# Moving early VectorE products to GpSimd and ScalarE, a later token weight, and w spread by a transfer, in a fused linear-attention and mixer kernel

## The chip, the cores and the metric

The kernel runs on one core of one Trainium2 chip. The metric is the device time of one execution in microseconds. Engine names are those of the profile: PE is TensorE (PEld its weight loads), DVE VectorE, ACT ScalarE, POOL GpSimd, SP SyncE, which only issues transfers here.

## The reference

Inputs r, k, v are (4 batches, 8 heads, 768 tokens, 48), w and u are (8, 48), all float32. A linear attention with decay runs over the tokens, and a mixer follows on its output:

```
for t in range(S):
    cur = einsum('bhd,bhe->bhde', u * k[t], v[t])
    y[t] = einsum('bhd,bhde->bhe', r[t], state + cur)
    state = w * state + einsum('bhd,bhe->bhde', k[t], v[t])
x = y as (B, 768, 384)
h = relu(x^T @ w_tok1) @ w_tok2        # over tokens, 768 -> 256 -> 768
u = x + h^T
out = u + relu(u @ w_ch1) @ w_ch2      # over channels, 384 -> 1536 -> 384
```

## The kernel before, in words

The attention is cut into 24 units of 128 tokens: six chunks of each of four batches. For a unit u the steps are these, by the names in the code:

- `kp`, `rp`: k and r (float32, as loaded) times powers of the decay, `wn` and `wp`, written as bfloat16 into `kpr`. The tables come from ln w: `lnw_` (line 618) takes logarithms of `w_ps` in PSUM into `lnw` (every row of which holds all of w) and `lnr` (r's layout), multiplies `lnr` by indices on DVE, and `wn_`, `wp_` take exponentials on ACT.
- `trk`, `trr`: PE transposes of the k and the r half into one PSUM tile `tr_ps`. `rk` copies both halves to SBUF on ACT after both are transposed; for units in `rk_two` (0 to 4 and 6) the copies are steps of their own, `rkk` behind `trk` and `rkr` behind `trr`.
- `at`: the scores of 8 heads into two PSUM tiles `at_ps` of four heads each. `AT0` and `AT1` multiply them by a causal mask on DVE, from PSUM. For units in `raw` (0, 1, 5, 8, 11) the second one is instead copied to SBUF as bfloat16 by ACT (`raw`) and masked from there (`ATr`).
- `pr`, `pg`, `yd`: the token's own term with u. `yS`, `y`: products with the state and with v, into `y_ps`. `x`: the sum, as `x_b`, read by the mixer. `kv`, `S`: the state; at the half of a batch `S` is multiplied by `wGm`, a product of a block mask `bm` and w to a power.

A planner (`Plan.run`, line 73) places all steps on the engines by assumed costs. The order in which it starts them is the program order; each engine then runs its list in order, and `fill` (line 130) puts idle matmuls into PE's planned gaps of the ramp. `products_in_turn` (line 146) makes some POOL products wait for a DVE step so that the two don't run against each other. The planned engine of `kp2` and `wGm` is DVE; `kp0`, `rp0`, `kp1`, `rp1`, `rp2`, `kp3` and most of the others of the first batch are on POOL.

Loads of the first six units are issued by SP in a fixed order from the start (`first_loads`, line 663), the next ones only after unit 5's y. The weights are transfers from POOL's queue (`weight`, line 694), in program order between its products: `w0` (first token weight) after `kp4`, `w1` (second token weight, `wtok2`) after `rp4`, and behind `rp5` five pieces of the channel weights, `w2`, `w6`, `w4` (first channel weight: a quarter, a quarter, a half), `w3`, `w5` (second channel weight, halves).

Spreading w: at line 536 ACT issues a transfer of w as one row of 384 into `row`, then one of four rows of 96 into `row4`. PE multiplies a column of ones by `row` (line 551) and a selection matrix `quarter` by `row4` (line 556) into `w_ps`, with idle matmuls around them.

The mixer of the first batch starts when its x is done: `hid` (tokens, first weight), `hr` (relu), then `ub` and `bk` with `wtok2`, then `z` with `wch1` in twelve pieces of 128 columns (pieces 0 to 2 read `w2`, 3 to 5 `w6`, 6 to 11 `w4`), `zr`, and `h` with `wch2`. PE's order is fixed by the plan, so a late weight stops PE.

Of the kernel before, what the change touches and what calls it, by code (L numbers as in the profile page):

```python
# [13 lines left out]
f32 = mybir.dt.float32  # L14
# [6 lines left out]
Ln = ACTF.Ln  # L21

B, H, S, D = 4, 8, 768, 48
# [22 lines left out]
class Plan:  # L46
# [83 lines left out]
    def fill(self, since, until, least, margin, each, emit):  # L130

        mine = sorted((s for s in self.steps if s.engine == "PE"), key=lambda s: s.start)
        for a, b in zip(mine, mine[1:]):
            if b.start > until:
                break
            if a.end < since:
                continue
            taken = sum(1 for x in self.used if x[0] < b.start and x[1] > a.end)
            n = int((b.start - a.end - margin) / each)
            if b.start - a.end >= least and taken < self.banks and n > 0:  # L140
                s = self.add(f"fill{a.name}", [("PE", n * each, n * each)], emit=emit(n))
                s.engine, s.start, s.end, s.seen = "PE", a.end, a.end + n * each, a.end + n * each
        return sorted(self.steps, key=lambda s: s.start)


def products_in_turn(steps, apart):


    both = [s for s in steps if s.engine in ("DVE", "POOL") and s.name.rstrip("0123456789") in ("kp", "rp", "ku", "rku", "yd", "wGm")]
    dve = [s for s in steps if s.engine == "DVE"]  # L150
    behind, d = {}, None
    for s in both:
        if s.engine == "DVE":
            d = s if len(s.after) and s.name[:2] != "yd" or s.ways[0][0] == "POOL" else d
        elif d is not None and s.start - d.end < apart:
            n = dve.index(d)
            behind[s] = dve[n - 1] if n and d.start - dve[n - 1].end < 0.05 else d
            d = None
    return behind
# [9 lines left out]
def graph(do, cfg):  # L169
# [246 lines left out]
CFG = dict(apart=2.0,   # L416
    transfers=[("u", u) for u in range(0, 6)]
    + [('k', 6)]
    + [('r', 6)]
    + [('k', 7)]  # L420
    + [('r', 7)]
    + [('v', 6)]
    + [('v', 7)]
    + [('u', 8)]
# [20 lines left out]
    xload={6: 0.33},  # L445
    wtime=(3.0, 2.6, 1.55, 5.2, 3.1, 3.9, 1.55),
    raw=(0, 1, 5, 8, 11),
    rk_two=(0, 1, 2, 3, 4, 6),
    mix=(0.0, 0.0, -1.0, -2.6),
    off3=[{}, {}, {'AT0': -0.12, 'rp': 0.83, 'rku': 1.35}],  # L450
# [17 lines left out]
def kernel(  # L468
# [15 lines left out]
    dm = H * D  # L484
# [8 lines left out]
    const = ctx.enter_context(tc.tile_pool(name="const", bufs=1))  # L493
# [7 lines left out]
    psM = ctx.enter_context(tc.tile_pool(name="psM", bufs=4, space=bass.MemoryType.PSUM))  # L501
# [19 lines left out]
    pe, dve, act, pool, sp = (InOrder(e) for e in (nc.tensor, nc.vector, nc.scalar, nc.gpsimd, nc.sync))  # L521
# [5 lines left out]

    idle = const.tile([128, 512], bf16, name="idle")
    dve.memset(idle, 0.0)
    row = const.tile([1, dm], f32, name="row")  # L530
    row4 = const.tile([HP, 2 * D], f32, name="row4")
    rows = const.tile([2 * HP, 2, P], f32, name="rows")
    dve.memset(rows, 1.0)
    wide = len(by_pe) < NU
    u_bc = const.tile([128, dm], f32, name="u_bc") if wide else None
    act.dma_start(out=row, in_=w.rearrange("h d -> (h d)")[None, :])
    act.dma_start(out=row4, in_=w.rearrange("(a q) d -> a (q d)", q=2))
    act.preload_act_table_set("natural_log_exp_and_others")
    ones = const.tile([1, 128], f32, name="ones")
    dve.memset(ones, 1.0)  # L540


    idle_ps = psM.tile([128, 512], f32, name="idle_ps", tag="m")
    w_ps = psM.tile([128, dm + 2 * D], f32, name="w_ps", tag="m")

    def warm(n):
        for _ in range(n):
            pe.matmul(idle_ps, idle[:, 0:128], idle, start=True, stop=True)

    warm(CFG.get("warm", (1, 10))[0])  # L550
    pe.matmul(w_ps[:, 0:dm], ones, row, start=True, stop=True, skip_group_check=True)
    ident = const.tile([128, 128], bf16, name="ident")
    make_identity(nc, ident)
    quarter = const.tile([HP, T // R, HP], f32, name="quarter")
    dve.tensor_copy(quarter, ident[0:HP, 0:HP].unsqueeze(1).to_broadcast([HP, T // R, HP]))
    pe.matmul(w_ps[:, dm:], quarter.rearrange("p t a -> p (t a)"), row4, start=False, stop=True, skip_group_check=True)
    warm(CFG.get("warm", (1, 10))[1])

    iota_i = const.tile([128, 2, G], i32, name="iota_i")
# [14 lines left out]
        out=mask, in_=mask, compare_op=ALU.is_gt,  # L574
# [15 lines left out]
    for i in range(NB):  # L590
        t = const.tile([128, 2, H, P], bf16, name=f"kpr{i}")
# [13 lines left out]
        dve.memset(S_i, 0.0)  # L605
        S0s.append(S_i)

    lnw = const.tile([128, dm], f32, name="lnw")
    wn = const.tile([128, G, dm], f32, name="wn")
    wp = const.tile([128, G, dm], f32, name="wp")  # L610
    wr = wp.rearrange("p g (q j d) -> p g q j d", q=2, j=R)
    lnr = const.tile([128, 2, D], f32, name="lnr")
# [3 lines left out]
    wGm = const.tile([128, HP, 2, D], f32, name="wGm")  # L616

    def lnw_(eng):
        act.activation(lnw, w_ps[:, 0:dm], Ln)
        act.activation(lnr.rearrange("p q d -> p (q d)"), w_ps[:, dm:], Ln)  # L620
        shape = [128, 2, R, D]
        for g in range(G):
            dve.tensor_mul(wr[:, g], lnr.unsqueeze(2).to_broadcast(shape), iota_r[:, g].unsqueeze(1).unsqueeze(3).to_broadcast(shape))
# [368 lines left out]
    def out_(eng, b, c, part, parts):  # L992
        sp.dma_start(out[b, ts(c, 128), ts(part, dm // parts)], M[b]["o", c, part])

    STEPS = {
        "lnw": lnw_, "wn": wn_, "wp": wp_, "wu": wu, "uw": uw, "ubc": ubc, "load": load, "weight": weight, "gd": gd, "wGm": wgm, "kp": kp, "rp": rp,
        "vb": vb, "ku": ku, "rku": rku, "adg": adg, "yd": yd, "turn_unit": turn_unit,
        "trk": lambda e, i: tr(0, i), "trr": lambda e, i: tr(1, i), "rk": rk, "at": at, "AT": AT, "raw": raw,
# [5 lines left out]
    def do(kind, *args):  # L1004
        return lambda eng: STEPS[kind](eng, *args)

    def fill(eng, n):
        t = psM.tile([128, 512], f32, name="fill_ps", tag="m")
        for lo in range(0, n, 2):
            cols = slice(0, 256 * min(2, n - lo))  # L1010
            pe.matmul(t[:, cols], idle[:, 0:128], idle[:, cols], start=True, stop=True)

    plan = graph(do, CFG)
    steps = plan.run()
    if CFG.get("fill"):
        first = next(s for s in steps if s.name == "z0_0_0").start
        steps = plan.fill(CFG.get("fill_from", 0.0), first, *CFG["fill"], lambda n: lambda eng: fill(eng, n))
    behind = products_in_turn(steps, CFG["apart"])
    last = {}
    for s in steps:  # L1020
# [38 lines left out]
```

## Time and profile before

| what | value |
|---|---|
| time, median of 3 runs | 165.36 us (164.93 to 165.66) |
| time of the profiled execution | 165.7 us |
| its span in the trace | 164.0 us |
| PE busy | 156.6 us (95%) |
| DVE busy | 109.2 us (67%) |
| ACT busy | 88.5 us (54%) |
| POOL busy | 67.1 us (41%) |
| first `z_ps` matmul | 29.94 us after the span's start |

Timeline lines give start, duration, engine, line, operation and tiles, then the count; a bracket holds the idle time before it and what ended it. Nearly all instructions have line 515, the helper that records them, so one goes by tiles: `kpr<-ld_k` is kp, `AT<-at_ps,mask` a masked score product, `AT<-raw,mask_b` the one from SBUF. Rows "A:B" of the stretches give the length, the busy time of PE, PEld, DVE, ACT and POOL (with counts), the granted clock, the DMA share and GB/s. Transfer lines end with the time from issue to landing.

### The profile page before, as it was taken

What the parts mean: (1) busy time and instruction counts of PE and PEld (TensorE: products, weight loads), DVE (VectorE), ACT (ScalarE), POOL (GpSimd) and SP (SyncE); (2) the same over time, 40 slices, a digit from 0 to 9 for tenths busy, and PEclk for the clock granted to TensorE, in tenths of its full rate; (3) what the DMA queues carried; (4) which work ended last, traced back from release to release, by engine and by line L of the source; (5) the groups of instructions that cost most, each with busy time, mean ns of one, the idle gap of its engine ahead of it and who ended that gap; (6) DMA issues with size and microseconds to landing.
All of it is one profiled execution on the core that took longest, in us unless ns stands there. A gap on an engine that the chain in (4) does not pass through costs nothing.

```text
span 164.0 us, 3852 instructions
## 1 busy us (share of the span) xinstructions
PE 156.6 (95%) x1466; PEld 100.9 (62%) x1466; DVE 109.2 (67%) x225; ACT 88.5 (54%) x194; POOL 67.1 (41%) x83
## 2 busy tenths in 40 slices
PE   6798999999999999899999999999999999999992
PEld 3277865566677666566566565666656655666562
DVE  6679897602289889899899899977876582012021
ACT  3898662595488466789706450077253502914900
POOL 8748893000037848566875856204750000000000
DMA  4999999999798997999999972999990028012012
GB/s 92 221 223 207 173 154 173 192 194 232 153 231 233 190 213 220 196 238 180 217 231 133 263 135 67 203 231 194 194 240 4 0 53 216 19 52 96 0 48 96
DMA packets 87307, 26.26 MB, mean 160 GB/s; under 512 B 76665, under 2 KB 87290, under 8 KB 87290
## 3 DMA queue, kind: packets, MB, share of 16 engines
q1 hardware_dynamic: 83392, 22.88, 65.1%
q0 software_dynamic: 3888, 3.15, 13.1%
q8 instruction: 11, 0.18, 0.4%
q14 instruction: 6, 0.05, 0.2%
q10 hardware_dynamic: 10, 0.00, 0.0%
HBM read 20.65 MB, written 4.72 MB: 155 GB/s over the span
## 4 chain that ended last, share of the span: by engine, by line
PE 85%; DVE 5%; ACT 5%; issue 2%; POOL 1%; DVEq 0%; ACTq 0%
PE h_ps L515 33%; PE z_ps L515 29%; PE y_ps L515 5%; PE at_ps L515 5%; PE tr_ps L515 4%; PE hT_ps L515 3%; PE kv_ps L515 3%; ACT rk L515 2%; DVE AT L515 2%; DVE x_b L515 1%; PE w_ps L515 1%; DVE yd L515 1%; POOL kpr L515 1%; ACT wp L515 1%; ACT raw L515 1%
## 5 line engine op out<-in xcount | busy, mean ns | idle before, releaser
L515 ACT ACTIVATE zr<-z_ps 128x384 bf16<-128x384 f32 x94 | 45.4, 492 | 44.2 <-PE z_ps L515 44.1
L515 PE MATMUL z_ps<-uT,wch 128*128 128x384 bf16 x288 | 52.5, 326 | 0.2
L515 PE MATMUL h_ps<-wch,zr 128*128 128x384 bf16 (+1 forms) x300 | 52.5, 320 | 0.0
L515 PEld LDWEIGHTS <-zr 128*128 128x128 bf16 x300 | 27.9, 98 | 15.5 <-issue 0.2
L515 PEld LDWEIGHTS <-wch 128*128 128x128 bf16 x288 | 26.7, 98 | 16.1 <-issue 0.4
L515 POOL TENSOR_TENSOR yd<-vb,adg 128x384 f32<-128x384 bf16 x18 | 15.5, 859 | 42.2 <-ACT adg L515 25.1
L515 DVE TENSOR_TENSOR AT<-at_ps,mask 128x512 bf16<-128x512 f32 x43 | 27.9, 683 | 0.6 <-PE at_ps L515 0.5
L515 DVE TENSOR_TENSOR osb<-u_sb,h_ps 128x384 f32<-128x384 bf16 (+1 forms) x22 | 11.7, 532 | 23.5 <-PE h_ps L515 23.4
L515 POOL TENSOR_TENSOR kpr<-ld_r,wp 128x384 bf16<-128x384 f32 x16 | 17.0, 1064 | 5.3 <-DVE yd L515 2.2
L515 ACT COPY rk<-tr_ps 128x512 bf16<-128x512 bf16 x28 | 15.5, 589 | 5.5 <-PE tr_ps L515 5.1
L515 PEld LDWEIGHTS <-kpr 128*128 128x128 bf16 x192 | 13.6, 108 | 6.1 <-POOL kpr L515 2.6
L515 DVE TENSOR_TENSOR x_b<-y_ps,yd 128x384 bf16<-128x384 f32 x24 | 13.3, 552 | 5.8 <-PE y_ps L515 5.5
L515 POOL TENSOR_TENSOR kpr<-ld_k,wn 128x384 bf16<-128x384 f32 x15 | 15.5, 1031 | 2.1 <-PE z_ps L515 1.1
L515 PEld LDWEIGHTS <-rk 48*128 48x128 bf16 (+1 forms) x272 | 11.1, 100 | 6.4 <-issue 2.8
L515 PE MATMUL tr_ps<-ident,kpr 128*128 128x128 bf16 x112 | 12.3, 247 | 2.0 <-ACT rk L515 1.0
L515 ACT CAST vb<-ld_v 128x384 bf16<-128x384 f32 x24 | 12.3, 511 | 3.5 <-DMA ld_v<-in_v_dram 3.5
L515 DVE TENSOR_TENSOR u_sb<-x_b,hT_ps 128x384 bf16<-128x384 bf16 x21 | 10.4, 546 | 1.1 <-PE hT_ps L515 1.1
L515 PEld LDWEIGHTS <-wtok 128*128 128x128 bf16 x90 | 8.0, 98 | 4.8 <-issue 0.6
L515 PEld LDWEIGHTS <-AT 128*128 128x128 bf16 x192 | 8.6, 99 | 3.6 <-DVE AT L515 0.7
L515 PE MATMUL at_ps<-rk 48*128 48x128 bf16 x192 | 10.4, 233 | 0.4 <-ACT rk L515 0.4
L515 DVE TENSOR_TENSOR kpr<-ld_k,wn 128x384 bf16<-128x384 f32 x9 | 5.9, 658 | 7.0 <-DMA ld_k<-in_k_dram 7.0
L515 PE MATMUL h_ps<-x_b,wtok 128*128 128x384 bf16 x48 | 10.2, 326 | 0.1
(91 smaller groups left out, 154.2 us busy)
## 6 DMA issues: line engine op xcount, KB each, us to landing
ld_k<-in_k_dram SPq DMA_DIRECT2D x24, 192.0 KB, 3.6
ld_v<-in_v_dram SPq DMA_DIRECT2D x24, 192.0 KB, 3.7
out_dram<-osb SPq DMA_DIRECT2D x23, 192.0 KB, 2.5
ld_r<-in_r_dram SPq DMA_DIRECT2D x28, 96.0 KB, 3.2
ld_r<-in_r_dram SPq DMA_DIRECT2D x10, 192.0 KB, 3.8
wch<-in_moe_w_ch_dram POOLq DMA_DIRECT2D x3, 576.0 KB, 12.6
wtok<-in_moe_w_tok_dram POOLq DMA_DIRECT2D x2, 384.0 KB, 5.1
wch<-in_moe_w_ch_dram POOLq DMA_DIRECT2D x2, 288.0 KB, 5.6
```

What stands on the lines that cost most here:

```text
L515: ins = tc.keep_in_program_order(f(*args, **kw))
```

## The change

Four things. `kp2` and `wGm` go from DVE to POOL, `wGm` directly ahead of `rp2`. The second masked product of units 2, 3 and 4 is done by way of `raw`, and unit 5's copy is split, `rkk` being put behind `trk` (and so ahead of `trr`). The transfer of the second token weight is put directly ahead of `w2`, behind `kp5` and `rp5`. And w is spread by a transfer that reads the row 128 times into `lnw`, whose logarithm is then taken in place, after that of `lnr`; the column of ones and its matmul are gone. The plan is made as before; `placed` edits its list afterwards, so no other step changes its place.

```
+def placed(steps, do, moved, raw, apart):
+    named = {s.name: s for s in steps}
+    for u in raw:
+        s = Step(f"raw{u}", [], (), None, (), 0.0, do("raw", u))
+        s.engine, s.start = "ACT", named[f"at{u}"].end + 0.001
+        s.end = s.seen = s.start + 0.6
+        named[f"AT1_{u}"].emit = do("ATr", u)
+        steps.append(s)
+    for u in apart:
+        s = Step(f"rkk{u}", [], (), None, (), 0.0, do("rkk", u))
+        s.engine, s.start = "ACT", named[f"trk{u}"].end + 0.001
+        s.end = s.seen = s.start + 0.5
+        named[f"rk{u}"].emit = do("rkr", u)
+        steps.append(s)
+    for name, engine, other in moved:
+        s, t = named[name], named[other]
+        s.engine = engine
+        if s is not t:
+            s.start = s.end = s.seen = t.start - 1e-6
+    return sorted(steps, key=lambda s: s.start)
...
+    raw_too=(2, 3, 4),
+    rk_apart=(5,),
+    moved=(('kp2', 'POOL', 'kp2'), ('wGm', 'POOL', 'rp2'), ('i:w1', 'POOL', 'i:w2')),
...
-    row = const.tile([1, dm], f32, name="row")
+    lnw = const.tile([128, dm], f32, name="lnw")
...
-    act.dma_start(out=row, in_=w.rearrange("h d -> (h d)")[None, :])
+    act.dma_start(out=lnw, in_=w.rearrange("h d -> (h d)")[None, :].to_broadcast([128, dm]))
     act.dma_start(out=row4, in_=w.rearrange("(a q) d -> a (q d)", q=2))
     act.preload_act_table_set("natural_log_exp_and_others")
-    ones = const.tile([1, 128], f32, name="ones")
-    dve.memset(ones, 1.0)
...
-    w_ps = psM.tile([128, dm + 2 * D], f32, name="w_ps", tag="m")
+    w_ps = psM.tile([128, 2 * D], f32, name="w_ps", tag="m")
...
-    pe.matmul(w_ps[:, 0:dm], ones, row, start=True, stop=True, skip_group_check=True)
...
-    pe.matmul(w_ps[:, dm:], quarter.rearrange("p t a -> p (t a)"), row4, start=False, stop=True, skip_group_check=True)
+    pe.matmul(w_ps, quarter.rearrange("p t a -> p (t a)"), row4, start=True, stop=True)
...
     def lnw_(eng):
-        act.activation(lnw, w_ps[:, 0:dm], Ln)
-        act.activation(lnr.rearrange("p q d -> p (q d)"), w_ps[:, dm:], Ln)
+        act.activation(lnr.rearrange("p q d -> p (q d)"), w_ps, Ln)
+        act.activation(lnw, lnw, Ln)
...
     steps = plan.run()
...
+    steps = placed(steps, do, CFG["moved"], CFG["raw_too"], CFG["rk_apart"])
     behind = products_in_turn(steps, CFG["apart"])
```

More of the change, by code (lines that the diff above doesn't have):

```diff
@@ L606 @@
         S0s.append(S_i)
-    lnw = const.tile([128, dm], f32, name="lnw")
     wn = const.tile([128, G, dm], f32, name="wn")
```

## The prediction

> **What bounds the kernel now.** I read the page first, then the busy times by stretch, then the chain that ended last, then the timeline of the first 40 us, then the landings of single transfers. The stretches carry the argument.
>
> ```profile
> span 164.0 us, 3852 instructions
> ...
> 5.00:10.00 5.00, 3.82 (x26) 2.25 (x25) 3.44 (x6) 4.51 (x10) 4.39 (x4) 1.00 1.06 219
> 10.00:14.00 4.00, 3.20 (x46) 2.59 (x43) 3.96 (x11) 3.92 (x11) 1.76 (x3) 1.00 1.00 220
> 14.00:19.80 5.80, 5.80 (x75) 4.84 (x75) 5.10 (x12) 4.07 (x9) 4.87 (x6) 1.00 0.89 184
> 19.80:28.00 8.20, 7.84 (x110) 5.26 (x108) 7.33 (x17) 3.50 (x9) 6.22 (x8) 1.00 1.21 159
> 28.00:40.00 12.00, 11.88 (x80) 7.22 (x80) 4.10 (x9) 9.41 (x20) 0.00 (x0) 1.00 1.23 201
> 40.00:80.00 40.00, 39.25 (x464) 26.76 (x463) 33.01 (x65) 28.09 (x66) 22.77 (x24) 1.00 0.94 208
> ```
>
> The columns after the length are PE, PEld, DVE, ACT, POOL. From 28 us on PE is busy for 99% and 98% of the two stretches shown: nothing that the change touches can shorten that, and what counts is when this part may begin. Ahead of it the bound moves: ACT with POOL (4.51 and 4.39 of 5.00) at 5 to 10, ACT (3.92 of 4.00) with DVE beside it at 10 to 14, PE (5.80 of 5.80) at 14 to 19.8, DVE (7.33 of 8.20, more than ACT or POOL, with PE padded by fill matmuls) from 19.8 to 28. The chain that ended last agrees at both ends of this ramp:
>
> ```profile
> 2.31 2.00 PE w_ps L515 x4
> ...
> 19.80 1.27 DVE AT L515 x2
> ```
>
> **Part 1: w by a transfer.** It removes the two-pass `w_ps<-row,ones` matmul and the `ones` memset. It adds a 192 KB transfer on ACT's queue, and turns the order round: `lnr` first, then `lnw`. The small `row4` transfer is issued behind the large one on the same queue, the quarter matmul waits for `row4`, and ACT takes `lnw` after `lnr`; so both landings are on the path.
>
> ```profile
> 0.81 0.80 ACTq L515 DMA_DIRECT2D row<-in_w_dram  x2
> 3.72 0.58 PE L515 MATMUL w_ps<-row,quarter 4*128 4x96 f32 x2
> 4.33 0.49 ACT L515 ACTIVATE lnw<-w_ps 128x384 f32<-128x384 f32 x1 [1.41 <-PE w_ps L515]
> 4.72 0.24 ACT L515 ACTIVATE lnr<-w_ps 128x96 f32<-128x96 f32 x1
> 4.85 0.62 ACT L515 ACTIVATE wn<-lnw,iota 128x384 f32<-128x384 f32 x1
> 5.61 1.27 POOL L515 TENSOR_TENSOR kpr<-ld_k,wn 128x384 bf16<-128x384 f32 x1 [0.99 <-POOL bm L515]
> ```
>
> ```profile
> ld_k<-in_k_dram SPq DMA_DIRECT2D x1, 192.0 KB, 2.8
> ```
>
> ```profile
> u_bc<-in_u_dram SPq DMA_DIRECT2D x1, 192.0 KB, 4.4
> ```
>
> No trace has this landing, so I bound it. Low: 2.31, when PE read the small `row`. High: the same broadcast of u behind other traffic, 0.81 + 4.4 = 5.21. Nearest is the first k load, as large and issued at the same 0.81: 3.61. I take 3.3, an estimate on the early side of it because nothing stands ahead in that queue. From there: quarter matmul 0.58 gives 3.88, `lnr` 0.03 after it (4.30 to 4.33 in the rows), `lnw` 0.13 to 0.24 behind `lnr`, `wn` 0.52 behind `lnw` (4.33 to 4.85): 4.56 to 4.67, and up to 4.94 if the first pass isn't loaded ahead. Before it was 4.85; I take a gain of 0.15. At the low end `wn` would stand at 3.6, but POOL is free only 0.99 ahead of 5.61, so 0.98 is the most. At the high end `wn` stands at 6.47 to 6.95, a loss of 1.6 to 2.1. The DVE products on `lnr` move with it. ACT is busy from there to 14 us but for some 0.5 of 9, so I let this shift reach PE's stretch whole.
>
> **Part 2: kp2 and wGm to POOL.**
>
> ```profile
> 10.64 0.55 DVE L515 TENSOR_TENSOR kpr<-ld_k,wn 128x384 bf16<-128x384 f32 x1
> ...
> 14.69 0.55 DVE L515 TENSOR_TENSOR wGm<-bm,wG 128x384 f32<-128x384 f32 x1
> ```
>
> ```profile
> 9.08 0.99 POOL L515 TENSOR_TENSOR kpr<-ld_r,wp 128x384 bf16<-128x384 f32 x1
> 12.31 1.13 POOL L515 TENSOR_TENSOR kpr<-ld_r,wp 128x384 bf16<-128x384 f32 x1 [2.24 <-DVE yd L515]
> ```
>
> ```profile
> 11.69 0.54 ACT L515 ACTIVATE wp<-wp 128x384 f32<-128x384 f32 x1
> ```
>
> ```profile
> 13.91 0.59 PE L515 MATMUL tr_ps<-ident,kpr 128*128 128x128 bf16 x4 [0.67 <-ACT rk L515]
> ```
>
> DVE loses two instructions of 0.55, about 1.0 start to start. POOL gains two in a gap of 2.24 (10.07 to 12.31). At 0.99 each they end at 12.05; at 1.27, as the product beside DVE's work at 5.61, at 12.6. rp2 starts when `wp` is done (11.69 + 0.54 = 12.23), so it is late by nothing to 0.4. Its transpose at 13.91 waits for ACT's copy of the k half and not for rp2, which ended at 13.44: over 0.4 of cover. So the move costs nothing, and the cover is just used up at the slow price. It also brings nothing by itself: the freed DVE time lies at 10 to 16, where ACT and then PE set the pace, and it turns into waiting for `rk` copies. [...]
>
> **Part 3: units 2, 3 and 4 by raw.** One masked product from PSUM becomes an ACT copy and a bf16 product. The price is read start to start:
>
> ```profile
> 11.10 0.68 DVE L515 TENSOR_TENSOR AT<-at_ps,mask 128x512 bf16<-128x512 f32 x1
> ...
> 12.16 0.42 DVE L515 TENSOR_TENSOR AT<-raw,mask_b 128x512 bf16<-128x512 bf16 x1
> 12.50 0.41 DVE L515 TENSOR_TENSOR pr<-tr_ps,rk 128x512 bf16<-128x512 bf16 x1
> ...
> 19.78 1.29 DVE L515 TENSOR_TENSOR AT<-at_ps,mask 128x512 bf16<-128x512 f32 x2
> 20.99 0.55 DVE L515 TENSOR_TENSOR yd<-vb,g_ps 128x384 f32<-128x384 bf16 x1
> ```
>
> ```profile
> 20.21 0.59 ACT L515 COPY rk<-tr_ps 128x512 bf16<-128x512 bf16 x1 [0.72 <-PE tr_ps L515]
> ...
> 22.58 1.07 ACT L515 COPY rk<-tr_ps 128x512 bf16<-128x512 bf16 x2 [1.23 <-PE tr_ps L515]
> ```
>
> Two PSUM products take 20.99 - 19.78 = 1.21. Half of that, 0.60, and 12.50 - 12.16 = 0.34 make 0.94: 0.27 less per unit. ACT has idle time of 0.72 and 1.23 for the copies of units 3 and 4 (0.59 each, about what these rows show). Unit 2 lies in PE's stretch and brings nothing. Unit 3, ahead of the DVE chain, brings 0.27, unit 4 another 0.27.
>
> **Part 4: unit 5's copies apart.** The row at 13.91 shows that the r transposes of a unit wait for the k copy when that copy stands between them.
>
> ```profile
> 19.79 0.38 PE L515 MATMUL tr_ps<-ident,kpr 128*128 128x128 bf16 x4
> ...
> 21.73 0.40 PE L515 MATMUL tr_ps<-ident,kpr 128*128 128x128 bf16 x4
> ```
>
> Before, both sets of transposes ran (first at 21.73), and both copies ended at 22.58 + 1.07 = 23.65, 1.92 after. Now: 0.40, ACT taken by raw4 until about 0.55, copy 0.59, transposes 0.40, copy 0.59: 2.2. That is 0.28 later against its own start, and eats unit 4's 0.27. Queued behind those waiting transposes on PE are yS4, the fills and y4. Sum of parts 3 and 4: 0.27, bounds 0 and 0.54.
>
> **Part 5: the second token weight behind rp5.**
>
> ```profile
> 19.32 0.78 POOL L515 DMA_DIRECT2D wtok<-in_moe_w_tok_dram  x1
> ...
> 22.03 4.02 POOL L515 DMA_DIRECT2D wch<-in_moe_w_ch_dram  x5
> ```
>
> ```profile
> wtok<-in_moe_w_tok_dram POOLq DMA_DIRECT2D x1, 384.0 KB, 4.8
> ```
>
> ```profile
> wch<-in_moe_w_ch_dram POOLq DMA_DIRECT2D x1, 288.0 KB, 5.3
> ```
>
> ```profile
> wch<-in_moe_w_ch_dram POOLq DMA_DIRECT2D x1, 576.0 KB, 9.3
> ```
>
> ```profile
> 18.37 0.99 POOL L515 TENSOR_TENSOR kpr<-ld_r,wp 128x384 bf16<-128x384 f32 x1 [0.48 <-DMA ld_r<-in_r_dram]
> ```
>
> ```profile
> 23.00:25.00 2.00, 1.80 (x27) 1.10 (x26) 1.83 (x5) 1.65 (x4) 2.00 (x3) 1.00 1.09 82
> ```
>
> ```profile
> 31.82 6.99 PE L515 MATMUL z_ps<-uT,wch 128*128 128x384 bf16 x42
> ```
>
> kp5 and rp5 move up by 0.78, but rp4 ahead of them waited for its r load, so they move no more. The second token weight is issued at about 21.25, lands 4.8 later at 26.05, and is read at 27.5 or so: covered by over 1 us. The five channel pieces are issued when they were, 22.03 on, but stand behind 384 KB more. The third is issued at 22.03 + 2 x 0.80 = 23.63 and landed at 32.9; its first reader is the fifth group of three in the row at 31.82 (14 groups, 0.50 each), at 33.8: 0.9 of cover. The delay of that stream is between nothing and 2.1 (384 KB at the 184 GB/s of 14 to 19.8). Two ways to narrow it: the slack of 23 to 25, where 82 GB/s moved and not 184, holds 0.20 MB of the 0.39, which leaves 1.0 us; or the first piece (288 KB, landed at 22.03 + 5.3 = 27.3) follows the token weight's landing at 26.05 at 201 GB/s, 1.5 later at 27.5, which leaves 0.2. I take 0.4, nearer to the second, since it is made of landings. Gain and delay together must stay under 0.9: 0.4 + 0.4 do, barely.
>
> **Sum.** 0.15 + 0.27 = 0.42, say 0.4, nothing lost behind it. The profiled execution took 165.7 (span 164.0 and 1.7 around it), 0.34 above the median of the three runs, 165.36. So 165.3 for a profile like it, and 165.0 for the median.
>
> **The rivals.** A measurement of this kernel can tell about 0.5% (0.8 us) from no change.
>
> *Early start, no cover lost* (164.5): the broadcast lands near 2.6, both units bring 0.27, and the weights are not delayed. The start is cut to 0.43 by the r load of unit 4 (rp4 can't start before 18.37, ends at 19.36, and is read at 19.79): 0.43 + 0.54 = 0.97, less 0.1 by what is left of the weights' delay. For it: only the first k load is issued as early as 0.81. Against it: that load needed 2.8.
>
> *The clock opens earlier* (164.3). Four transposes take 0.59 at 13.91, 0.38 at 19.79 and 0.40 at 21.73, though the column of granted clock says 1.00 throughout: PE turned fast at about 19.8, after 5.9 us without the gap that the row at 13.91 shows. If it turned some 3 us earlier, PE's stretch would shrink until DVE (5.10 of its 5.80) bound it: 0.7 on top of 0.4. [...]
>
> *Nothing is left* (165.4): 0.15 doesn't come, or the third channel piece comes 0.4 later than I take.
>
> *Slower, the channel weights* (166.6): the whole 2.1 is added to the stream. The third piece lands at 35.0, and PE, in its fixed order, stands at the seventh group from 33.8 on: 1.2 lost, and no work fills it. It decides from a delay of 0.9 on, and over 0.8 us from 1.7. Against it: the slack at 23 to 25.
>
> *Slower, the transfer* (166.7): it lands at 5.21 as u's did, `wn` is 1.6 late, less 0.27. It costs over 0.8 from a landing of about 4.4 on. Against it: u's ran behind a full queue.
>
> That kp2's move or the split copies don't do what they say is in the bounds above: both are worth nothing here.
>
> **How the numbers follow.** Forecast 0.46, early start 0.21, clock 0.09, nothing left 0.08, channel weights 0.08, transfer 0.08. Faster is 0.21 + 0.09 = 0.30, within 0.5% is 0.46 + 0.08 = 0.54, slower 0.16. The forecast's own range is 164.5 to 165.5. For 8 in 10 I go down to 164.0, which takes in the two faster cases, and up to 166.0, which leaves out the two slower ones.
>
> **What would show it.** Right: `wn` first at 4.5 to 4.9, both POOL products done by 12.7, the transposes of unit 2 still waiting for `rk`, unit 3's `yd` about 0.27 closer to its first AT, the fifth unit's r transposes released by `rk`, the first `z_ps` 0.4 earlier, no PE idle between 32 and 36. Wrong: `lnw` waiting for a DMA past 4.4; PE idle ahead of a `z_ps` and released by a DMA; transposes at 0.4 before 17; or a PE gap after 28 that grows by what the ramp saved.

## The result and the profile after

The changed kernel takes 167.53 us (median of 4 runs, 167.41 to 168.0) where the kernel before takes 165.47 (4 runs): a ratio of 1.0129, with a 95% interval of 1.0105 to 1.0152. That is slower by 2.1 us, and outside the predicted range. The profiled execution took 167.41, its span 165.7 us, 1.7 longer than before.

The stretches of the kernel after, with the same columns as those of before (length; PE, PEld, DVE, ACT, POOL; granted clock, DMA share, GB/s):

```profile
5.00:10.00 5.00, 3.68 (x17) 1.98 (x18) 1.97 (x4) 3.89 (x9) 2.74 (x3) 1.00 0.97 212
10.00:14.00 4.00, 3.75 (x40) 2.71 (x39) 3.09 (x8) 3.73 (x11) 3.24 (x5) 1.00 0.96 207
14.00:19.80 5.80, 5.12 (x71) 4.33 (x66) 5.80 (x11) 4.75 (x10) 5.78 (x6) 1.00 0.95 206
19.80:28.00 8.20, 7.24 (x118) 5.25 (x117) 7.70 (x17) 5.54 (x13) 6.91 (x9) 1.00 0.88 118
28.00:40.00 12.00, 11.88 (x87) 7.07 (x84) 4.28 (x10) 8.70 (x19) 0.00 (x1) 1.00 1.24 199
```

From 28 us on nothing has changed: PE is busy for 99%, as before. The loss lies in the ramp. From 5 to 10 POOL has fallen from 4.39 to 2.74 and DVE from 3.44 to 1.97: the start is late. From 14 to 19.8 DVE has 11 instructions instead of 12 and is busy for all of the 5.80 (5.10 before). Work was taken from it, and it became the bound. PE was that before.

The timeline of the first 8 us of the kernel after shows the late start (the recording helper is line 540 now):

```profile
0.81 0.42 ACTq L540 DMA_DIRECT2D lnw<-in_w_dram  x1
1.26 0.59 ACTq L540 DMA_DIRECT2D row<-in_w_dram  x1
2.65 1.90 SPq L540 DMA_DIRECT2D ld_r<-in_r_dram  x1
5.06 0.71 PE L540 MATMUL w_ps<-row,quarter 4*128 4x96 f32 x2 [2.75 <-DMA row<-in_w_dram]
5.80 0.25 ACT L540 ACTIVATE lnr<-w_ps 128x96 f32<-128x96 f32 x1 [2.63 <-PE w_ps L540]
5.95 0.52 ACT L540 ACTIVATE lnw<-lnw 128x384 f32<-128x384 f32 x1
6.50 0.61 ACT L540 ACTIVATE wn<-lnw,iota 128x384 f32<-128x384 f32 x1
```

The DMA issues of its first 1.25 us (size, then us from issue to landing):

```profile
lnw<-in_w_dram ACTq DMA_DIRECT2D x1, 192.0 KB, 3.7
ld_k<-in_k_dram SPq DMA_DIRECT2D x1, 192.0 KB, 4.5
```

And the first long piece of its chain that ended last (start, length):

```profile
1.26 3.66 DMA row<-in_w_dram
```

The large transfer lands at 0.81 + 3.7 = 4.5, the small one behind it at 1.26 + 3.66 = 4.92, and `wn` starts at 6.50 instead of 4.85. The k load beside it takes 4.5 instead of 2.8. One issue of SP's lasts 1.90, where the issue at that time took 0.59 before; every load behind it is issued later.

Next, the timeline of POOL's and DVE's products in the kernel after:

```profile
11.12 1.17 DVE L540 TENSOR_TENSOR UW<-wu_sb 64x4 bf16<-64x4 f32 x2
11.27 0.99 POOL L540 TENSOR_TENSOR kpr<-ld_k,wn 128x384 bf16<-128x384 f32 x1
...
15.90 1.00 POOL L540 TENSOR_TENSOR kpr<-ld_r,wp 128x384 bf16<-128x384 f32 x1
15.94 1.25 DVE L540 TENSOR_TENSOR AT<-raw,mask_b 128x512 bf16<-128x512 bf16 x1
...
18.91 1.01 POOL L540 TENSOR_TENSOR kpr<-ld_r,wp 128x384 bf16<-128x384 f32 x1
18.97 1.23 DVE L540 TENSOR_TENSOR AT<-raw,mask_b 128x512 bf16<-128x512 bf16 x1
...
21.21 1.00 POOL L540 TENSOR_TENSOR kpr<-ld_k,wn 128x384 bf16<-128x384 f32 x1 [1.29 <-DMA ld_k<-in_k_dram]
21.99 0.50 DVE L540 TENSOR_TENSOR AT<-raw,mask_b 128x512 bf16<-128x512 bf16 x1
```

`AT<-raw,mask_b`, 0.41 to 0.42 in the rows of before, takes 1.25 and 1.23 here, and each time a POOL product runs beside it. POOL's ends at 15.90 + 1.00 = 16.90, DVE's 0.29 later; POOL's at 19.92, DVE's 0.28 later. The two tiny `UW` products (4 columns) last from 11.12 to 12.29, POOL's kp2 until 12.26. It looks as if these DVE products can end only when POOL is done. Who starts first matters: unit 0's product, 0.14 ahead of rp2, takes its 0.42 at 13.71, and rp2 takes 1.15 instead of 0.99.

Last, the kernel after at the transposes of unit 5 and at the first z:

```profile
24.42 0.38 PE L540 MATMUL tr_ps<-ident,kpr 128*128 128x128 bf16 x4 [0.79 <-ACT rk L540]
25.46 0.42 DVE L540 TENSOR_TENSOR pr<-tr_ps,rk 128x512 bf16<-128x512 bf16 x1 [0.31 <-ACT rk L540]
...
31.63 0.65 PE L540 MATMUL z_ps<-uT,wch 128*128 128x384 bf16 x3
```

By then the two traces stood closer: `yd` of unit 3 is 1.42 later than before, that of unit 4 1.17. But unit 5's r transposes come at 24.42 (22.14 before), and the first z at 31.63, 1.69 late. That is the loss of the span.

### The profile page after: what moved, and what is told of

It is laid out like the page before. It is cut to its first block, busy times and chain, and to the rows that moved or that the text cites. A ratio compares the mean times of both kernels' runs of the same rounds, so it can differ in the third digit from the quotient of the medians.

```text
span 165.7 us, 3844 instructions
## 1 busy us (share of the span) xinstructions
PE 154.7 (93%) x1464; PEld 99.8 (60%) x1464; DVE 108.8 (66%) x222; ACT 90.0 (54%) x197; POOL 68.5 (41%) x85
## 4 chain that ended last, share of the span: by engine, by line
PE 82%; DVE 7%; ACT 4%; DMA 2%; issue 2%; POOL 1%; ACTq 0%; POOLq 0%; DVEq 0%
PE h_ps L540 34%; PE z_ps L540 28%; PE at_ps L540 5%; PE y_ps L540 5%; PE hT_ps L540 3%; PE tr_ps L540 3%; DVE AT L540 3%; PE kv_ps L540 2%; DMA row<-in_w_dram 2%; ACT rk L540 1%; DVE x_b L540 1%; DVE yd L540 1%; DVE pr L540 1%; POOL kpr L540 1%; DVE UW L540 1%
## 5 line engine op out<-in xcount | busy, mean ns | idle before, releaser
L540 DVE TENSOR_TENSOR AT<-at_ps,mask 128x512 bf16<-128x512 f32 x40 | 26.1, 683 | 0.6 <-PE at_ps L540 0.5
L540 POOL TENSOR_TENSOR kpr<-ld_k,wn 128x384 bf16<-128x384 f32 x16 | 16.5, 1034 | 5.2 <-ACT wn L540 2.6
L540 DVE TENSOR_TENSOR kpr<-ld_k,wn 128x384 bf16<-128x384 f32 x8 | 5.4, 674 | 7.7 <-DMA ld_k<-in_k_dram 7.7
```

The lines of the kernel that those rows point to most:

```text
L540: ins = tc.keep_in_program_order(f(*args, **kw))
```

## The experiments

Three causes were in question: the transfer, the POOL products beside DVE, and the split copies. Each could have carried the whole loss, or the later token weight could have. In the tables below "first z" is the start of the first `z_ps` matmul in the profiled run (29.94 before). It is one execution: the moment from which PE's small instructions become fast (four transposes 0.6, then 0.4) lies near 17 us in some of these traces and past 20 in others (0.39 at 17.37 in `moves_in_turn_raw4`, still 0.56 at 20.45 in `rest_no_split`), so a few tenths of first z say little alone, and the medians decide.

### Which part costs what

| kernel | median us | ratio (95%) | first z |
|---|---|---|---|
| w_transfer_only | 166.64 | 1.0067 (1.0043 to 1.0091) | 30.67 |
| rest_only | 166.45 | 1.0059 (1.0039 to 1.0079) | 30.87 |
| rest_no_split | 165.83 | 1.0036 (1.0017 to 1.0054) | 30.12 |
| row4_first | 166.32 | 1.0053 (1.0031 to 1.0075) | 30.52 |

`w_transfer_only`, against after:

```
-    raw_too=(2, 3, 4), rk_apart=(5,),
-    moved=(('kp2', 'POOL', 'kp2'), ('wGm', 'POOL', 'rp2'), ('i:w1', 'POOL', 'i:w2')),
+    raw_too=(), rk_apart=(), moved=(),
```

> The kernel before with only the transfer of w in place of the matmul. Theory A (the transfer is the whole loss; the other three edits give back what they gain): wn first at 6.4 to 6.6 as in the changed kernel, first z matmul 1.6 to 1.8 later than before, 1.6 to 2.1 us slower. Theory B (the other edits cost too, the POOL moves by slowing DVE beside them): wn as late, but the time only 1.0 to 1.4 us slower than before.

`rest_only`, against after (the matmul with `ones` and the order of before are back):

```
-    act.dma_start(out=lnw, in_=w.rearrange("h d -> (h d)")[None, :].to_broadcast([128, dm]))
+    act.dma_start(out=row, in_=w.rearrange("h d -> (h d)")[None, :])
```

> The changed kernel with w spread by the matmul as before: the POOL moves, the raw units, the split of unit 5 and the later token weight alone. Theory A: within 0.4 us of before, since raw's gain at units 3 and 4 (0.46 in the changed kernel) is lost at unit 5's r transposes. Theory B: 0.4 to 0.9 us slower than before, with bf16 masked products of 1.2 us beside POOL products on DVE.

The two halves cost 0.67% and 0.59%, 1.1 and 1.0 us of 165.5. Their sum is 2.1, what the whole change costs. Neither half is the whole cause. Theory B came closest in both: 1.1 lies in its 1.0 to 1.4, and 1.0 just above its 0.4 to 0.9. In `w_transfer_only` `wn` stands at 6.21, 1.36 late, but the first z is only 0.73 late. PE's instructions become fast between 19.1 and 19.8 after the start in both traces (before: eight score products 0.61 at 19.14, four transposes 0.38 at 19.79; here: four transposes 0.63 at 19.09, eight products of `y` 0.36 at 19.84, which took 0.53 at 18.68 before), so with a later start less of the work runs at the slow rate. This would explain the difference, but no run isolates it.

`row4_first`, against after: row4's transfer goes ahead of the large one.

```
-    act.dma_start(out=lnw, in_=w...to_broadcast([128, dm]))
     act.dma_start(out=row4, in_=w.rearrange("(a q) d -> a (q d)", q=2))
+    act.dma_start(out=lnw, in_=w...to_broadcast([128, dm]))
```

> The changed kernel with the two transfers of w issued in the other order, the four-row one first. Theory C (queue order: row4 stood behind the large transfer): quarter matmul done by 3.5, lnr by 3.6, lnw at its own landing of 4.5, wn at about 5.1, so 1.2 to 1.4 us faster than the changed kernel. Theory D (the large transfer takes the DMA engines from the first loads, whatever its place in its queue): the first k load still lands near 5.3 and later loads stay 1.3 to 2 us late, so 0.3 to 0.9 us faster than the changed kernel at most.

From its timeline, and from its DMA issues:

```profile
2.28 0.71 PE L540 MATMUL w_ps<-row,quarter 4*128 4x96 f32 x2
...
4.77 0.52 ACT L540 ACTIVATE lnw<-lnw 128x384 f32<-128x384 f32 x1 [1.43 <-DMA lnw<-in_w_dram]
5.32 0.61 ACT L540 ACTIVATE wn<-lnw,iota 128x384 f32<-128x384 f32 x1
...
35.30 0.99 PE L540 MATMUL z_ps<-uT,wch 128*128 128x384 bf16 x5 [0.78 <-DMA wch<-in_moe_w_ch_dram]
```

```profile
ld_k<-in_k_dram SPq DMA_DIRECT2D x1, 192.0 KB, 2.9
```

The quarter matmul now runs at 2.28, and `wn` is 1.18 earlier than in after. The median falls by 1.2. So the order on the one queue made most of the transfer's loss, as Theory C had it. Theory D expected the first k load to stay as late as in after; with the large transfer issued 0.6 later it lands 2.9 after its issue, not 4.5. Yet `lnw` still waits for the large transfer until 4.77, and before it began at 4.33, on what the matmul had spread. In neither order did the transfer bring w to ACT before the matmul did. The last line of the timeline is new: PE waits 0.78 for a channel weight. This profile is of the slowest of the ten runs (167.21), so the wait need not be in the others.

### Why the transfer lands late

Two kernels add a 192 KB transfer to the kernel before, at the head of ACT's queue, into a tile that is loaded anew before it is read. `extra_same_row` reads w's row 128 times, `extra_own_rows` 128 rows of a weight. Theory S is that the repeated row is slow; Theory T is that any such transfer there delays what is behind and beside it.

```
+    act.dma_start(out=u_bc, in_=w.rearrange("h d -> (h d)")[None, :].to_broadcast([128, dm]))   # extra_same_row
+    act.dma_start(out=u_bc, in_=moe_w_ch1[0:128, 0:dm])                                         # extra_own_rows
     act.dma_start(out=row, in_=w.rearrange("h d -> (h d)")[None, :])
```

> The kernel before, with one more transfer ahead of w's two on ACT's queue: 128 times the same row of w into a tile that is loaded anew before it is read. Theory S (128 reads of one row are slow): lands about 3.7 us after its issue, first k load at 5.2 to 5.3 as in the changed kernel, the SP queue's fourth issue held up as there. Both theories: w's own rows land behind it, lnw about 7, 2 to 3 us slower.

> The same with 128 different rows of the channel weight, as many bytes in as large pieces. Theory S: lands in some 2.8 us like the first k load of before, the first k load near 4.3, and 0.7 to 1.2 us faster than extra_same_row. Theory T (192 KB ahead of the first loads cost that whatever they read): the same landings and the same time as extra_same_row within 0.3 us.

The first DMA issues of `extra_same_row`, then of `extra_own_rows`:

```profile
u_bc<-in_w_dram ACTq DMA_DIRECT2D x1, 192.0 KB, 3.8
ld_k<-in_k_dram SPq DMA_DIRECT2D x1, 192.0 KB, 4.6
```

```profile
u_bc<-in_moe_w_ch_dram ACTq DMA_DIRECT2D x1, 192.0 KB, 2.7
ld_k<-in_k_dram SPq DMA_DIRECT2D x1, 192.0 KB, 3.5
```

Their timelines, where PE gets the small row behind the transfer (same row first):

```profile
2.65 2.02 SPq L540 DMA_DIRECT2D ld_r<-in_r_dram  x1
...
4.10 1.61 PE L540 MATMUL w_ps<-row,ones 1*128 1x384 f32 x2 [1.79 <-DMA row<-in_w_dram]
```

```profile
2.64 0.84 SPq L540 DMA_DIRECT2D ld_r<-in_r_dram  x1
...
4.30 1.61 PE L540 MATMUL w_ps<-row,ones 1*128 1x384 f32 x2 [2.00 <-DMA row<-in_w_dram]
```

Theory S has the landings right: the repeated row costs 1.1 us, to itself and to the k load, and it is what stretches SP's issue (2.02 against 0.84). Theory T has the times right: 167.95 and 167.93 us, 1.0149 (1.0118 to 1.0179) and 1.0145 (1.0112 to 1.0177), first z 31.67 in both. The small row, read at 2.31 before, is there at 4.10 and 4.30, whatever the transfer ahead of it reads. So a large transfer ahead of a small one on the queue was enough for the loss in both runs. A large one on another queue was not: the first k load was issued at the same 0.81 in the kernel before, where the row was there at 2.31. Nor does the small one wait for all of the large one: in `extra_same_row` it is there at 4.10, the large one at 0.81 + 3.8 = 4.6. What holds it, beyond the order, isn't shown. For `lnw` itself, as the change reads it, the repeated row counts besides.

### POOL's products and DVE

| kernel | median us | ratio (95%) | first z |
|---|---|---|---|
| pool_moves_only | 166.4 | 1.0043 (1.0019 to 1.0066) | 30.58 |
| pool_moves_in_turn | 165.41 | 0.9987 (0.9968 to 1.0005) | 29.97 |
| raw34_only | 166.24 | 1.0040 (1.0016 to 1.0064) | 30.47 |
| raw34_in_turn | 165.43 | 1.0018 (0.9997 to 1.0039) | 29.68 |
| raw4_only | 165.15 | 0.9978 (0.9960 to 0.9995) | 29.63 |

All of these spread w as before. `pool_moves_only` has the two moves alone:

```
+    raw_too=(), rk_apart=(),
+    moved=(('kp2', 'POOL', 'kp2'), ('wGm', 'POOL', 'rp2')),
```

> The kernel before with kp2 and wGm on POOL and nothing else. Theory B (a DVE product whose two inputs both lie in SBUF waits until the POOL product beside it has ended, so more POOL work slows DVE): UW ends with kp2 at about 11.1, later than the 10.27 of before, the masked product of unit 0 from raw takes 0.9 to 1.2 us instead of 0.42 beside rp2, and the kernel is 0.2 to 0.5 us slower. Theory A (the moves are neutral, as predicted): within 0.15 us of before.

`pool_moves_in_turn` has the same, and three POOL products wait for the DVE product that they would run against:

```
     behind = products_in_turn(steps, CFG["apart"])
+    named = {s.name: s for s in steps}
+    behind[named["kp2"]] = named["uw"]
+    behind[named["rp2"]] = named["AT1_0"]
+    behind[named["rp3"]] = named["AT1_1"]
```

> pool_moves_only with three waits added on POOL: kp2 behind UW, rp2 behind the product from raw of unit 0, rp3 behind that of unit 1. Theory B (port): UW done by 10.4, that product of unit 0 at 0.42, pr0 at about 10.3, and most of the 0.7 us that pool_moves_only lost comes back: within 0.25 us of before. If POOL's longer list is what cost, the waits on it make the kernel slower still, 0.7 us or more above before.

"Port" is the author's name for Theory B: the traces show when these products end, and not what holds them.

The timeline of `pool_moves_only` around kp2, then that of `pool_moves_in_turn`:

```profile
9.73 1.47 DVE L540 TENSOR_TENSOR UW<-wu_sb 64x4 bf16<-64x4 f32 x2
10.18 0.99 POOL L540 TENSOR_TENSOR kpr<-ld_k,wn 128x384 bf16<-128x384 f32 x1
...
11.23 0.42 DVE L540 TENSOR_TENSOR pr<-tr_ps,rk 128x512 bf16<-128x512 bf16 x1
```

```profile
9.54 0.68 DVE L540 TENSOR_TENSOR UW<-wu_sb 64x4 bf16<-64x4 f32 x2
10.25 0.42 DVE L540 TENSOR_TENSOR pr<-tr_ps,rk 128x512 bf16<-128x512 bf16 x1
10.35 1.00 POOL L540 TENSOR_TENSOR kpr<-ld_k,wn 128x384 bf16<-128x384 f32 x1 [0.33 <-DVE UW L540]
```

The POOL moves alone cost 0.4%, 0.7 us, more than the 0.2 to 0.5 that Theory B gave. `UW` ends at 11.20, kp2 at 11.17; with kp2 behind it, `UW` ends at 10.22 and `pr` starts 0.98 earlier, of which 0.19 is an earlier start of `UW`. With the waits the loss is gone, though not every delay is: unit 0's product from `raw`, 1.10 in `pool_moves_only`, still takes 0.73 beside `wGm`, where 0.42 was expected. POOL does the same work in both kernels, so the loss is from what runs at the same time, and not from POOL having more to do. Nor did the move gain: by its interval `pool_moves_in_turn` can't be told from no change.

`raw34_only` has units 3 and 4 by `raw` and no move (`raw_too=(3, 4)`); `raw34_in_turn` adds a wait of rp5 for unit 3's masked product; `raw4_only` has unit 4 alone (`raw_too=(4,)`).

```
+    behind[named["rp5"]] = named["AT1_3"]      # raw34_in_turn only
```

> The kernel before with units 3 and 4 by way of raw. Theory A (0.27 less DVE time for each, wherever POOL stands): 0.3 to 0.5 us faster. Theory B (port): unit 3's product from raw meets kp5 on POOL and takes about 1 us, which gives its gain back and more; unit 4's meets only the issue of weights, takes 0.42 and brings 0.27: within 0.3 us of before.

> raw34_only with rp5 on POOL made to wait for unit 3's product from raw. Theory B (port): that product ends with kp5, 0.6 to 1.0 us instead of 1.69, and 0.4 to 0.8 us of the 0.7 that raw34_only lost comes back. If the extra ACT copy of unit 3 were the cost, the time stays with raw34_only's, 0.5 to 0.8 us above before.

> The kernel before with unit 4 alone by way of raw; POOL issues transfers at that time and multiplies nothing. Theory B (port): the product from raw takes 0.42, yd follows 0.27 closer, 0.1 to 0.3 us faster than before. If raw itself is what made raw34_only slow, 0.2 us slower or more.

Timeline of `raw34_only` at unit 3, then of `raw4_only` at unit 4:

```profile
19.57 0.68 DVE L540 TENSOR_TENSOR AT<-at_ps,mask 128x512 bf16<-128x512 f32 x1
19.61 1.01 POOL L540 TENSOR_TENSOR kpr<-ld_k,wn 128x384 bf16<-128x384 f32 x1
20.16 1.69 DVE L540 TENSOR_TENSOR AT<-raw,mask_b 128x512 bf16<-128x512 bf16 x1
20.57 0.99 POOL L540 TENSOR_TENSOR kpr<-ld_r,wp 128x384 bf16<-128x384 f32 x1
```

```profile
22.79 0.42 DVE L540 TENSOR_TENSOR AT<-raw,mask_b 128x512 bf16<-128x512 bf16 x1
```

The first fence has both kinds of DVE product beside kp5 (19.61 to 20.62). The one from PSUM (`at_ps`) takes its usual 0.68. The one from SBUF (`raw`) takes 1.69: it ends at 21.85, when kp5 is done and rp5 too (21.56). Unit 4's comes when POOL only issues weight transfers, and takes 0.42. So unit 4 alone gains 0.2%, 0.36 us, and with unit 3 added the kernel is 0.7 slower than before. Theory B had it within 0.3: it took the hold for about 1 us. In after the hold was short: kp5 had waited 1.29 for its late load and was nearly done when unit 3's product started, which took 0.50 and ended 0.28 behind kp5.

In `raw34_in_turn` unit 3's product takes 1.20, above the 0.6 to 1.0 expected. Of what `raw34_only` lost, 0.8 comes back by the medians and 0.4 by the ratios, so the hold was at least part of the loss. The profiled run gets its first z 0.26 before the kernel before, and is no faster. Its z from 34.26 on had waited:

```profile
34.26 1.96 PE L540 MATMUL z_ps<-uT,wch 128*128 128x384 bf16 x11 [0.58 <-DMA wch<-in_moe_w_ch_dram]
```

The third channel piece landed at about 34.2 here and at 32.9 before, though it was issued only 0.06 later. Its landing changed by 1.3 us between these two traces, of kernels that leave the order of the weights alone. (This run took 166.18, and eight of the kernel's twelve 165.39 to 165.48.)

### The split and the second token weight

`rest_no_split` is `rest_only` with `rk_apart=()`; `split_only` is the kernel before with `rk_apart=(5,)` alone; `w1_only` has only `moved=(('i:w1', 'POOL', 'i:w2'),)`.

> As rest_only, but unit 5's two copies stay together behind both transposes. Theory A (the split ate raw's gain): 0.3 to 0.5 us faster than rest_only, 0.2 to 0.4 faster than before. Theory B (products on POOL slow DVE's): no more than 0.2 faster than rest_only.

> The kernel before with unit 5's copies apart. Theory A (as predicted, the last copy ends 0.3 later against its transposes): 0.2 to 0.4 us slower. Theory E (PE's order doubles it: yS4, fills, y4 and at5 stand behind the waiting transposes): 0.5 to 0.8 us slower, as rest_only stood 0.62 behind rest_no_split.

> The kernel before with the second token weight issued behind rp5. As predicted: kp5 and rp5 some 0.7 earlier, which nothing on the DVE chain waits for, the token weight landed by 26.6 and not waited for: within 0.2 us of before. The rival (the channel weights come late): PE idle ahead of a z matmul between 33 and 36, released by a DMA, 0.3 to 1.2 us slower.

`split_only` takes 165.55 us, 0.9996 (0.9980 to 1.0011), first z 29.62; `w1_only` 165.65, 1.0012 (0.9998 to 1.0027), first z 29.74. Neither can be told from no change, so both theories on `split_only`, slower by 0.2 or more, failed. `rest_no_split` fits neither of its own: it is faster than `rest_only`, as Theory A has it, but not faster than before. `rest_only` is above `rest_no_split` by 0.62 in the medians, 0.4 by the ratios, whose intervals overlap. Unit 5 in the timeline of `rest_only`, then of `rest_no_split`:

```profile
22.54 0.59 ACT L540 CAST raw<-at_ps 128x512 bf16<-128x512 f32 x1 [0.95 <-PE at_ps L540]
23.02 0.59 ACT L540 COPY rk<-tr_ps 128x512 bf16<-128x512 bf16 x1
23.66 0.38 PE L540 MATMUL tr_ps<-ident,kpr 128*128 128x128 bf16 x4 [0.78 <-ACT rk L540]
...
24.70 0.42 DVE L540 TENSOR_TENSOR pr<-tr_ps,rk 128x512 bf16<-128x512 bf16 x1 [0.31 <-ACT rk L540]
```

```profile
22.70 0.38 PE L540 MATMUL tr_ps<-ident,kpr 128*128 128x128 bf16 x4
23.12 1.07 ACT L540 COPY rk<-tr_ps 128x512 bf16<-128x512 bf16 x2
...
24.22 0.42 DVE L540 TENSOR_TENSOR pr<-tr_ps,rk 128x512 bf16<-128x512 bf16 x1
```

With the split PE goes transposes, ACT copy, transposes, ACT copy, and unit 4's `raw` copy at 22.54 stands in front of the first copy on ACT. Unit 5's r transposes come 0.96 later, its `pr` 0.48. Of either, 0.24 was there already at unit 4's `yd` (23.85 and 23.61). Alone the split has no `raw` in front, and the same wait (0.60 in `split_only`) is hidden. That `raw4` makes the difference rests on these three kernels; unit 4's `raw` with the split and nothing else wasn't run.

`w1_only` at the third channel piece:

```profile
34.14 3.10 PE L540 MATMUL z_ps<-uT,wch 128*128 128x384 bf16 x18 [0.41 <-DMA wch<-in_moe_w_ch_dram]
```

The piece landed at 34.2, 1.3 later than before, of which 0.28 is the later issue. The z had begun 0.2 earlier and the wait took that back. Since the section before saw such a landing with the token weight in its old place, not all of the 1.3 is shown to come from the move.

### What was left that gains

`moves_in_turn_raw4` has the POOL moves with their three waits and `raw` for unit 4, and w, the token weight and unit 5's copies as before:

```
+    raw_too=(4,), rk_apart=(),
+    moved=(('kp2', 'POOL', 'kp2'), ('wGm', 'POOL', 'rp2')),
...
+    behind[named["kp2"]] = named["uw"]
+    behind[named["rp2"]] = named["AT1_0"]
+    behind[named["rp3"]] = named["AT1_1"]
```

> pool_moves_in_turn and raw4_only together, w by the matmul, no split, the token weight where it was. If their effects add (0.13% and 0.22%): 0.4 to 0.8 us faster than before. If both only free the same DVE time: 0.1 to 0.4 us faster, as raw4_only.

It takes 164.87 us (12 runs, 164.61 to 165.2), 0.9972 of before (0.9956 to 0.9988), first z 29.20, and PE waits for no weight. The gain of 0.46 is as if the two effects added, but by its interval (0.2 to 0.7) it can't be told from the 0.36 of `raw4_only`. It is the fastest of these kernels, 2.7 us below the change as made.

## Why the prediction was wrong

**Part 1, the landing.** The step that failed first is "I take 3.3", one landing for both transfers. The large one took until 4.5, the small one until 4.92, within the bounds of 2.31 and 5.21 but at the other end. Two sizes were wrong in it. The row chosen as nearest, the first k load's 2.8, is of a transfer that reads 128 different rows: `extra_own_rows` has such a one land after 2.7 in this very place, and the repeated row costs 1.1 more. And the small transfer, which the prediction saw to stand behind the large one, was given no time for it: it is there 1.8 to 2.0 later behind either kind. The k load pays as well, 4.5 instead of 2.8. The mechanism was seen: the rival "the transfer" had `wn` 1.6 late (measured 1.65) and a threshold of 4.4 for the landing (measured 4.5), but was given 0.08. Its reason for the lateness, other traffic, was only a part. And "I let this shift reach PE's stretch whole" was too much: alone, 1.36 at `wn` cost 1.1.

**Part 2, "the move costs nothing".** This step was wrong in its mechanism. It asked what POOL's products cost beside DVE (1.27 against 0.99) and never what DVE's cost beside POOL. `UW` and the masked products from SBUF are on the way to `pr`, `g` and `yd`, and took longer where a POOL product had started first (in `pool_moves_only` 1.47 for `UW`, before 0.69 at 9.58, and 1.10 for unit 0's product, before 0.42 at 12.16): 0.7 us of that kernel's time. The idle gap of POOL was no free place. Where the inputs lie goes with it: in `raw34_only` the product with both in SBUF took 1.69, beside kp5 and rp5, and the one with one in PSUM 0.68, beside kp5. What makes the first wait is not shown.

**Part 3.** 0.27 per unit was right for unit 4 (0.36 measured, 0.08 to 0.66 by the interval), and unit 3's product keeps its 0.42 only where no POOL product holds it (0.42 in `rest_no_split`, 1.69 in `raw34_only`). The price came from a row of `AT<-raw` (12.16) that started 0.15 ahead of the POOL product beside it (12.31).

**Part 4.** The split was to eat 0.28. Alone it cost nothing measurable; with unit 4's `raw` ahead of it the kernel is 0.4 to 0.6 slower than without it, by intervals that overlap. Its mechanism was as foretold: the r transposes are released by `rk`. Parts 3 and 4 brought no gain: `rest_only` loses 1.0, more than the 0.7 of the POOL moves alone.

**Part 5.** Nearly right: no measurable cost alone. The delay, taken as 0.4, was 1.3 in the trace of `w1_only`, which used up the cover of 0.9, though not all of it is shown to come from the move. In the changed kernel PE waits for no weight because all else is 1.7 late: the third piece lands at about 35.4, and its first reader has moved from 33.8 to about 35.5.

**The sum.** No rival had two losses at once. The transfer rival's 166.7 and the 0.7 of the POOL moves make 167.4, near the 167.5 that was measured, but by some luck: that rival counted 1.6 for the transfer and a gain of 0.27, where the runs show 1.1 and no gain. Two of the prediction's sums are off by up to 0.1, which decides nothing: by its own steps the high end of `wn` is 6.85, not 6.95, and the terms of part 4 make 2.13, not 2.2. PE didn't turn fast earlier: four transposes still take 0.57 at 19.66 in the kernel after. In other traces here it did: in that of `moves_in_turn_raw4` they take 0.39 at 17.37, 2.4 ahead of 19.79. The "some 3 us" of *The clock opens earlier* was the author's supposition, which no run shows. That it is a clock isn't shown either: the granted clock is 1.00 in every stretch from 5 to 40 us, in both kernels.

## What to carry to other kernels

Before a product goes to GpSimd, list the VectorE instructions beside which it will run, and look at where their inputs are: here those with both inputs in SBUF took longer where it had started first (1.69 instead of 0.42 in `raw34_only`), and waits that put the two in turn were cheaper than the overlap (165.41 us in `pool_moves_in_turn`, 166.4 in `pool_moves_only`). A duration taken from a row holds only with that row's neighbours (the first k load took 2.8 before, and 4.5 after with the transfer of w beside it): ask what ran beside it on POOL, DVE or the DMA engines, and whether the change keeps that so. A small transfer that is needed first goes ahead of a large one on its queue: in `row4_first` that took 1.2 us off the median.

## What the runs showed of the hardware

In the kernel after, a DVE product with both inputs in SBUF that began while a POOL product ran ended after it: by 0.03 for `UW`'s 4 columns (12.29, POOL's 12.26), and by 0.28 and 0.29 for 512 (20.20 and 19.92, 17.19 and 16.90). In `raw34_only` two POOL products in a row held it (1.69); in the kernel after, at 15.94, it came through behind one, and the next on POOL took 1.20. Reading one row 128 times landed 1.1 us later than reading 128 rows (3.8 in `extra_same_row` and 2.7 in `extra_own_rows`, for 192 KB), and on the other queue the first k load and one issue took longer too (4.6 against 3.5, and 2.02 against 0.84).
